# Routed attention and experts: the first pair loaded, turned and masked in halves, the key masks moved to ScalarE, and several experts' sums reordered

## The chip, the cores and the metric

The kernel runs on one core of a Trainium2 chip. The metric is the device time of one execution in microseconds, as the median of three runs. The engines are named as the profile names them: PE is TensorE (its weight loads are PEld), DVE is VectorE, ACT is ScalarE, POOL is GpSimd, and SP is SyncE, which here issues most of the DMAs.

## What is computed

Attention in which a query sees only the keys of its own cluster, followed by a layer of eight experts in which each token goes to one expert. The reference, cut to what matters:

```python
# q, k, v: (4, 8, 768, 64); centroids: (8, 16, 64)
q_n, k_n, c_n = (t / (np.linalg.norm(t, axis=-1, keepdims=True) + 1e-06) for t in (q, k, centroids))
q_assign = np.argmax(np.einsum('bhsd,hcd->bhsc', q_n, c_n), axis=-1)
k_assign = np.argmax(np.einsum('bhsd,hcd->bhsc', k_n, c_n), axis=-1)
mask = q_assign[:, :, :, None] == k_assign[:, :, None, :]
scores = np.where(mask, scale * np.matmul(q, k.transpose(0, 1, 3, 2)), -1000000000.0)
attn = softmax(scores)
x = np.matmul(attn, v)            # then (B,H,S,D) -> (3072 tokens, 512)
# experts: w_gate (512, 8), w1 (8, 512, 1024), w2 (8, 1024, 512)
expert_idx = np.argmax(x @ w_gate, axis=1)
y[token] = gate_w * (np.maximum(x[token] @ w1[e], 0.0) @ w2[e])   # e = expert_idx[token]
```

## The kernel before

The order of instructions on every engine is the order in which the program writes them (a manual schedule). Work that is to run beside other work is hung on hooks: `at_pair(n, u, f)` runs `f` after score step `u` of pair `n`, and in the experts `at(h1, i, f)` and `at(h2, i, f)` run `f` at hook `i` of layer 1 or layer 2 of stage `s`.

**Attention** goes over 16 pairs: a pair `n` is one batch and two heads, whose 2 x 64 dimensions fill the 128 partitions. For each pair:

- `load(n)` brings q and k. For pairs after the first it uses 128-byte pieces, in an order that lets DVE turn them in 32 x 32 blocks (`turn`, L277). Pair 0 is loaded by four DMAs on the SP and ACT queues (L183) in 256-byte pieces and is turned by 12 PE transposes into PSUM (L267), from where DVE and ACT copy it (`first_turn`, L282).
- `prepare(n, 1)` is `similar` (L312): the products of q and k with the normed centroids `cT`. `assign0`, `assign1` and `assign2` (L325 to L348) are seven DVE operations over 384 columns: turn, maximum, comparison, rank, maximum, comparison, turn. They end in `ohT`, the one-hot cluster of every query and key.
- `place` (L359, L361) spreads `ohT` into the masks: `mq` for queries by ACT copies, `mk` for keys by DVE, which multiplies by 2^60 and subtracts 2^60. Four instructions each, of 32 x 384.
- Twelve scores (`score`, L379, L392): for each half `h` of the queries and each block `j` of 128 keys, PE forms q times k in f32 (two passes, one of each head beside the other) and adds the bf16 product `mk` times `mq` to the same PSUM tile; ACT takes Exp of it. In pair 0 the first three raw products are issued before the first mask product. `add_up` (L398, DVE) sums the Exp tiles. There are three PSUM tiles for scores (`ps_s`) and two for everything else (`ps_m`).
- `attend` (L404): 24 products of the Exp tiles with v, then two ACT copies into `oT` (L411). `sum_up` (L427) for pair n runs at step 2 of pair n + 1, and so does `similar` for pair n + 2.

While a pair is computed, the next pair's `similar` is at step 2, `assign0` and `assign1` at 5, `assign2` at 7, `place` for keys at 8 and for queries at 11 (for pair 0's successor `similar` is at 4).

After the last pair of a batch the tokens are given to experts: `gate`, `gate_exp`, `choose`, `count` (L539 and L540: two f32 products with 128 x 128 constants of zeros and ones) and `number`, which scatters the tokens' rows by POOL (L554).

**Experts** run in ten stages (`s` from 0 to 9), each one expert's rows: layer 1 by Strassen-Winograd with 7 products for each of two halves (`layer1`, L916), layer 2 likewise for whole pairs of 128 rows (L1017), and directly for the rest (L1036). The sums that Strassen needs of weights (`w1_sums`, `w2_sums`) and of rows (`x_sums`, `h_sums`) are DVE operations of line L736; the additions that end a product are L874. For stage s + 1 and later ones: `places` reads the token list (`sf`) through SP, `indices` makes offsets of it on DVE, `gather` fetches rows by POOL (L685), `weigh` scales them on DVE (L702) and stores them, `take` reads them back, and `turn_rows` (L727) turns them. `ask` and `answer` check that all sums are in range.

## Time and profile before

| What | us |
|---|---|
| Median of three runs (lowest to highest) | 670.79 (670.62 to 671.94) |
| The profiled execution, its own time | 672.25 |
| Its span, first to last instruction | 670.7 |
| First PE instruction after the span's start | 5.24 |
| Attend of pair 0 begins | 27.32 |
| One ordinary pair, attend to attend | 19.74 |
| Last attend ends, experts begin | 336.5 |

The profile is of one execution, which took 1.5 us longer than the median. A group line names source line, engine and operation, what is written from what, how often, the busy time with the mean of one in ns, and the idle time of the engine just before it with what ended it. In a timeline the columns are start and length in us, engine, line and operation; brackets give the idle time ahead and its releaser. Ends of matmuls are modelled, so distances between starts are the better measure on PE.

### The profile page before, as it was taken

The numbers are of one execution on the slowest core, as the hardware profiler recorded it, in microseconds if no ns is written. First come the engines' busy times: TensorE is split into PE (matmuls) and PEld (weight loads), VectorE is DVE, ScalarE is ACT, GpSimd is POOL, SyncE is SP. The second block draws the span as 40 slices with busy tenths as digits, with TensorE's granted clock in tenths as the row PEclk, the third lists the DMA queues.
The fourth block names the chain that finished last, engine by engine and source line by source line (L and its number), as shares of the span: only waits on it lengthen the run. The fifth ranks groups of instructions, "written<-read, shape, count | busy, mean of one in ns | idle before, by whom it ended". The sixth has DMA issues, their size and how long they took to land.

```text
span 670.7 us, 11366 instructions
## 1 busy us (share of the span) xinstructions
PE 649.9 (97%) x4210; PEld 425.7 (63%) x4210; DVE 512.3 (76%) x901; ACT 300.0 (45%) x522; POOL 127.3 (19%) x156
## 2 busy tenths in 40 slices
PE   5999999999999999999999999999999999999995
PEld 2444444454444455444575879989798887969773
DVE  5889999999999999999886868878778366572300
ACT  3666556657556565556622333243332331423210
POOL 4100000012000300033104704225240422130010
PEclk9899999999999999999999989999999999999998
DMA  6843455433455443347475586685675844625010
GB/s 118 191 86 72 82 95 95 66 73 72 77 95 95 65 81 73 70 115 239 115 266 142 189 297 217 253 321 156 275 239 229 261 160 138 221 93 182 8 48 18
DMA packets 191806, 95.36 MB, mean 142 GB/s; under 512 B 155967, under 2 KB 173887, under 8 KB 190464
## 3 DMA queue, kind: packets, MB, share of 16 engines
q1 hardware_dynamic: 184560, 81.15, 44.0%
q0 software_dynamic: 4928, 12.97, 5.8%
q8 instruction: 35, 0.57, 0.4%
q10 hardware_dynamic: 2256, 0.44, 0.4%
q14 instruction: 27, 0.22, 0.1%
HBM read 74.10 MB, written 20.70 MB: 141 GB/s over the span
## 4 chain that ended last, share of the span: by engine, by line
PE 77%; issue 9%; DVE 7%; POOL 2%; DMA 2%; ACT 1%; POOLq 0%; SPq 0%; DVEq 0%; ACTq 0%
PE sps L379 20%; PE mps L404 15%; PE bank L916 9%; PE sbank L916 7%; PE bank L1017 7%; PE bank L1036 7%; PE sbank L1017 5%; PE mps L427 2%; PE mps L312 2%; DMA xg<-x_rows,gi 1%; PE bank L885 1%; DVE acc L398 1%; DVE v L736 1%; DVE xT L727 1%; POOL tokens_of L554 1%
## 5 line engine op out<-in xcount | busy, mean ns | idle before, releaser
L392 ACT ACTIVATE A<-sps 128x768 f32<-128x768 f32 x192 | 153.5, 811 | 44.9 <-PE sps L379 44.1
L379 PE MATMUL sps<-qT,kT 64*128 64x384 f32 x768 | 159.3, 494 | 0.6 <-ACT A L392 0.6
L398 DVE TENSOR_TENSOR acc<-acc,A 128x768 f32<-128x768 f32 x128 | 121.4, 948 | 10.1 <-ACT A L392 2.8
L404 PE MATMUL mps<-A,v_in 128*64 128x384 f32 x768 | 127.4, 488 | 0.0
L379 PEld LDWEIGHTS sps<-qT,kT 64*128 64x128 f32 x768 | 67.1, 188 | 55.0 <-issue 51.4
L404 PEld LDWEIGHTS mps<-A,v_in 128*64 128x64 f32 x768 | 53.8, 137 | 70.5 <-issue 61.7
L991 POOL DMA_INDIRECT out_dram<-z,si x30 | 47.6, 1587 | 198.4 <-DVE z L874 169.3
L554 POOL DMA_INDIRECT tokens_of<-tg,pos_i x24 | 26.7, 1111 | 281.9 <-DVE pos_i L552 148.2
L379 PE MATMUL sps<-mq,mk 64*128 64x384 bf16 x384 | 63.5, 325 | 2.6 <-DVE mk L361 2.6
L1036 PE MATMUL bank<-w,h 128*128 128x512 f32 (+2 forms) x224 | 64.4, 596 | 0.0
L685 POOL DMA_INDIRECT xg<-x_rows,gi x30 | 42.7, 1423 | 48.2 <-DVE si L676 18.1
L359 ACT COPY mq<-ohT 32x384 bf16<-32x384 bf16 x62 | 31.6, 510 | 42.7 <-DVE ohT L348 41.8
L916 PE MATMUL sbank<-xc,a 128*128 128x144 f32 (+4 forms) x288 | 48.0, 310 | 0.2
L916 PE MATMUL bank<-xT,w 128*128 128x144 f32 (+4 forms) x288 | 47.8, 309 | 0.0
L874 DVE TENSOR_TENSOR h<-sbank,p 128x288 f32<-128x288 f32 (+4 forms) x18 | 9.2, 512 | 48.3 <-PE sbank L916 48.3
L916 PEld LDWEIGHTS bank<-xT,w 128*128 128x128 f32 x288 | 43.8, 191 | 2.6 <-issue 2.2
L1036 PEld LDWEIGHTS bank<-w,h 128*128 128x128 f32 (+2 forms) x224 | 24.7, 152 | 32.5 <-issue 32.3
L916 PEld LDWEIGHTS sbank<-xc,a 128*128 128x128 f32 x288 | 43.3, 191 | 0.9 <-ACT sbank L940 0.6
L379 PEld LDWEIGHTS <-mk 64*128 64x128 bf16 x384 | 19.5, 95 | 28.0 <-DVE mk L361 3.4
L934 ACT ACTIVATE h<-h 128x288 f32<-128x288 f32 (+4 forms) x36 | 17.6, 488 | 42.7 <-DVE h L874 42.5
L702 DVE TENSOR_TENSOR xw<-xg,sf 128x256 f32<-128x256 f32 (+2 forms) x60 | 32.8, 606 | 1.8 <-DMA xg<-x_rows,gi 1.6
L398 DVE TENSOR_TENSOR acc<-A 128x768 f32<-128x768 f32 x32 | 30.2, 945 | 3.1 <-ACT A L392 2.9
(208 smaller groups left out, 890.7 us busy)
## 6 DMA issues: line engine op xcount, KB each, us to landing
w<-in_moe_w_dram SPq DMA_DIRECT2D x20, 2048.0 KB, 12.0
v_in<-in_v_dram SPq DMA_DIRECT2D x32, 192.0 KB, 2.8
x_rows<-x SPq DMA_DIRECT2D x64, 96.0 KB, 2.4
turn_rows<-xw SPq DMA_DIRECT2D x23, 256.0 KB, 2.0
q_in<-in_q_dram SPq DMA_DIRECT2D x60, 96.0 KB, 3.2
k_in<-in_k_dram SPq DMA_DIRECT2D x60, 96.0 KB, 3.2
xs<-turn_rows SPq DMA_DIRECT2D x16, 144.0 KB, 2.8
xs<-turn_rows SPq DMA_DIRECT2D x8, 208.0 KB, 4.2
```

Source lines behind the costliest of these rows:

```text
L359: (nc.gpsimd.tensor_copy if n == 0 and h else nc.scalar.copy)(dst, src)
L379: nc.tensor.matmul(SP[n, h, j][:, a, 0:HS], lhsT=kt[rows, j * P : (j + 1) * P], rhs=qt[rows, h * HS : (h + 1) * HS], start=first, stop=not ...
L392: nc.scalar.activation(A[n, h, j], ps[:, :, 0:HS], AF.Exp, scale=D**-0.5)
L398: nc.vector.tensor_tensor(ACC[n, h], first, A[n, h, j], op=ALU.add)
L404: nc.tensor.matmul(O[n, h][D * a : D * (a + 1), 0:HS], lhsT=VIN[n][:, a, j, :], rhs=A[n, h, j][:, a, :], start=(j == 0), stop=(j == NQ - 1),)
L554: ins = nc.gpsimd.indirect_dma_start(out=t_d[:, :], out_offset=bass.IndirectOffsetOnAxis(ap=pos_i[:, i : i + 1], axis=0), in_=tg[:, b, i, ...
L685: nc.gpsimd.indirect_dma_start(out=xg[0:m], out_offset=None, in_=x_d[0:rows_in, :], in_offset=bass.IndirectOffsetOnAxis(ap=g["gi"][0:m, j ...
L702: nc.vector.tensor_tensor(xw[0:m, :, :, d2 * a : d2 * (a + 1)], xg[0:m].rearrange("p (r a d b) -> p a r b d", r=HP, a=2, b=DB)[:, a], g["s ...
L916: nc.tensor.matmul(ps[:, f * T2 : (f + 1) * T2], lhsT=w[:, k, (2 * j + f) * P : (2 * j + f + 1) * P], rhs=x[:, k, :], start=first and f + ...
L991: ins = nc.gpsimd.indirect_dma_start(out=out[:, :], out_offset=bass.IndirectOffsetOnAxis(ap=GR[s]["si"][0:rows, j : j + 1], axis=0), in_=z ...
L1017: nc.tensor.matmul(ps[:, 0:H], lhsT=x[:, k, :], rhs=y[:, k, :], start=first and k == 0, stop=k == 3, skip_group_check=not first,)
L1036: nc.tensor.matmul(ps[i * m : (i + 1) * m, :], lhsT=h[:, f, j * P : j * P + m], rhs=w[:, f, :], start=(k == 0), stop=(k == FB // n - 1),)
```

## The change

Loading and turning pair 0: q and k come in four DMAs on SP's queue, the first half (of each partition's six rows) of q, of k, then the second halves, in pieces of 768 bytes. v of pair 0, the loads of pair 1 and the two small gate-weight loads follow on the same queue, ahead of the stores of `cT`, which used to be first. Six bf16 products of zeros are issued on PE before anything else. The halves are turned by products with the identity instead of transposes, copied by ACT alone, and clustered one after the other in chains over 192 columns. The masks of each half are placed by ACT, DVE and GpSimd together; GpSimd takes half of the key masks and most query masks. The three raw scores ahead are placed between the two halves.

All later pairs: the key masks are placed by ACT (Identity with a per-partition scale and bias) at step 11 instead of by DVE at step 8. Pair 1's preparation in pair 0 is moved to steps 6, 7, 8 and 11.

Counting: the constants and the operand are bf16 instead of f32.

Experts: the order of the `x_sums`, the hooks of some weight sums, of `places`, `ask` and `answer`.

The diff, cut to its core:

```diff
+        nc.gpsimd.tensor_copy(lt_b, lt_strict)
+        nc.gpsimd.memset(ones_b, 1.0)
...
-                if n == 0:
-                    t = d[n] = t.rearrange("p i d -> p (i d)").rearrange("p (j a d) -> p j a d", a=2, d=D)
-                    for a in range(2):
-                        (nc.sync, nc.scalar)[a].dma_start(out=t[:, :, a, :], in_=src[0, a].rearrange("(p j) d -> p j d", j=NQ))
-                    continue
...
+        def load_first():
+            for d, name in ((QIN, "q_in"), (KIN, "k_in")):
+                d[0] = ld.tile([P, NI, Q4], F32, name=name).rearrange("p i d -> p (i d)").rearrange("p (a j d) -> p a j d", a=2, d=D)
+            for h in range(2):
+                js = slice(NQ // 2 * h, NQ // 2 * (h + 1))
+                for d, src in ((QIN, q), (KIN, k)):
+                    nc.sync.dma_start(out=d[0][:, :, js, :], in_=src[0, 0:2].rearrange("a (p j) d -> p a j d", j=NQ)[:, :, js, :])
...
-        load(0)
+        load_first()
+        load_v(0)
+        load(1)
...
+        for t in (MQ[0], MK[0]):
+            nc.vector.memset(t, 0.0)
...
+        idle = ps_s.tile([P, 2, 512], F32, name="sps")
+        for _ in range(6):
+            nc.tensor.matmul(idle[:, 0, :], lhsT=MQ[0][:, 0:P], rhs=MQ[0][:, 0:512], start=True, stop=True)
...
-        warm = consts.tile([P, 1], F32)
-        nc.scalar.activation(warm, cnrm, AF.Exp, scale=0.0)
...
-            nc.scalar.dma_start(
+            nc.sync.dma_start(
...
-        nc.vector.tensor_tensor(cinv, cinv, cs2, op=ALU.mult)
-        nc.vector.tensor_tensor(cinv, cinv, cnrm, op=ALU.add)
+        nc.vector.tensor_scalar(cinv, cinv, scalar1=cs2[:, 0:1], scalar2=cnrm[:, 0:1], op0=ALU.mult, op1=ALU.add)
...
-        for d in (QIN, KIN):
-            ps = ps_s.tile([P, 2, 512], F32, name="sps")
-            t = d.pop(0)
-            for j in range(NQ):
-                c0 = P * (j % 3)
-                nc.tensor.transpose(ps[:, j // 3, c0 : c0 + P], t[:, j].rearrange("p a d -> p (a d)"), ident)
-            first.append(ps)
-            if d is QIN:
-                nc.tensor.transpose(cps[:, 0:P], cn.rearrange("p a d -> p (a d)"), ident)
...
-        first_turn(0)
-        cv = cps[:, 0:P].rearrange("p (h a c) -> p h a c", a=2, c=C)
-        for a in range(2):
-            nc.vector.tensor_copy(cT[D * a : D * (a + 1), :, a, :], cv[D * a : D * (a + 1), :, a, :])
...
-        load_v(0)
-        load(1)
-        first_turn(1)
...
+        def assign0(n, part=1):
+            sim = asg.tile([P, HI, 2 * C], F32, name="sim")[:, 0 : HI // part]
+            nc.vector.transpose(sim.rearrange("p i c -> p (i c)"), SIM.pop(n)[:, 0 : HS // part])
...
-            OH[n] = asg.tile([P, HS], BF16, name="ohT")
+            OH[n] = asg.tile([P, HS], BF16, name="ohT")[:, 0 : HS // part]
             nc.vector.transpose(OH[n], oh.rearrange("p i c -> p (i c)"))
...
                     if w == 0:
-                        (nc.gpsimd.tensor_copy if n == 0 and h else nc.scalar.copy)(dst, src)
+                        nc.scalar.copy(dst, src)
                     else:
-                        nc.vector.tensor_scalar(
-                            dst, src, scalar1=ksc2[Q4 * g : Q4 * (g + 1), a : a + 1],
-                            scalar2=kscn2[Q4 * g : Q4 * (g + 1), a : a + 1], op0=ALU.mult, op1=ALU.add,
-                        )
+                        big, less = (t[Q4 * g : Q4 * (g + 1), a : a + 1] for t in (ksc2, kscn2))
+                        nc.scalar.activation(dst, src, AF.Identity, bias=less, scale=big)
...
+        def start_first():
+            HQ = HS // 2
+            cps = ps_m.tile([P, 512], F32, name="mps")
+            ps = [ps_s.tile([P, 2, 512], F32, name="sps") for _ in range(2)]
+            src = [d.pop(0) for d in (QIN, KIN)]
+            dst = [qkt.tile([P, S], F32, name=name) for name in ("qT", "kT")]
+            QT[0], KT[0] = dst
+            def turned(w, h):
+                for j in range(NQ // 2):
+                    for a in range(2):
+                        nc.tensor.matmul(
+                            ps[w][D * a : D * (a + 1), h, P * j : P * (j + 1)], lhsT=src[w][:, a, NQ // 2 * h + j, :], rhs=ident,
+                            start=True, stop=True,
+                        )
+            def copied(w, h):
+                nc.scalar.copy(dst[w][:, HS * h : HS * (h + 1)], ps[w][:, h, 0:HS])
+            def similar_half(h):
+                sps = SIM[0] = ps_m.tile([P, 512], F32, name="mps")
+                for g in range(4):
+                    c0 = HS * h + HQ * (g % 2)
+                    nc.tensor.matmul(
+                        sps[Q4 * g : Q4 * (g + 1), 0:HQ], lhsT=cT[:, 0].rearrange("p a c -> p (a c)"),
+                        rhs=dst[g // 2][:, c0 : c0 + HQ], start=True, stop=True,
+                    )
+            def place_half(h, w):
+                for g in (2 * w, 2 * w + 1):
+                    for a in range(2):
+                        c0 = HS * h + HQ * (g % 2)
+                        to = (MQ, MK)[w][0][D * a : D * a + Q4, c0 : c0 + HQ]
+                        rows = slice(Q4 * g, Q4 * (g + 1))
+                        if w == 0:
+                            (nc.gpsimd.tensor_copy if h or g else nc.scalar.copy)(to, OH[0][rows])
+                        else:
+                            (nc.gpsimd if g % 2 else nc.vector).tensor_scalar(
+                                to, OH[0][rows], scalar1=ksc2[rows, a : a + 1], scalar2=kscn2[rows, a : a + 1],
+                                op0=ALU.mult, op1=ALU.add,
+                            )
+            def clusters(h):
+                assign0(0, 2)
+                assign1(0, 2)
+                assign2(0, 2)
+                for w in (h, 1 - h):
+                    place_half(h, w)
+            turned(0, 0)
+            copied(0, 0)
+            turned(1, 0)
+            copied(1, 0)
+            warm = consts.tile([P, 1], F32)
+            nc.scalar.activation(warm, cnrm, AF.Exp, scale=0.0)
+            nc.tensor.transpose(cps[:, 0:P], cn.rearrange("p a d -> p (a d)"), ident)
+            cv = cps[:, 0:P].rearrange("p (h a c) -> p h a c", a=2, c=C)
+            for a in range(2):
+                nc.vector.tensor_copy(cT[D * a : D * (a + 1), :, a, :], cv[D * a : D * (a + 1), :, a, :])
+            turned(0, 1)
+            copied(0, 1)
+            similar_half(0)
+            turned(1, 1)
+            copied(1, 1)
+            clusters(0)
+            score_half(0, 0, 0, True)
+            similar_half(1)
+            for j in (1, 2):
+                score_half(0, 0, j, True)
+            clusters(1)
+            OH.pop(0)
+            for a in range(2):
+                nc.sync.dma_start(
+                    out=cn_d.rearrange("(h a) d c -> a d h c", a=2)[a], in_=cT[D * a : D * (a + 1), :, a, :]
+                )
...
-            ahead = range(3) if n + h + j == 0 else (j,) if n + h or j > 2 else ()
-            for i in ahead:
-                score_half(n, h, i, True)
+            if n + h or j > 2:
+                score_half(n, h, j, True)
...
-            last = LAST[b] = rt.tile([P, E], F32, name="last")
+            last = LAST[b] = rt.tile([P, E], BF16, name="last")
...
-            nc.tensor.matmul(cps[:, 0:E], lhsT=lt_strict, rhs=last, start=True, stop=True)
-            nc.tensor.matmul(cps[:, E : 2 * E], lhsT=ones_sq, rhs=last, start=True, stop=True)
+            nc.tensor.matmul(cps[:, 0:E], lhsT=lt_b, rhs=last, start=True, stop=True)
+            nc.tensor.matmul(cps[:, E : 2 * E], lhsT=ones_b, rhs=last, start=True, stop=True)
...
+            strassen(V, X[2], b22, b12, ALU.subtract)
             strassen(V, X[0], b12, b11, ALU.subtract)
             strassen(V, X[1], b22, X[0], ALU.subtract)
-            strassen(V, X[2], b22, b12, ALU.subtract)
             strassen(V, X[3], b21, X[1], ALU.subtract)
...
-            for u, step in ((2 if n else 4, 1), (5, 2), (7, 3), (8, 4), (11, 5)):
+            for u, step in ((2 if n else 6, 1), (5 if n else 7, 2), (7 if n else 8, 3), (11, 4), (11, 5)):
...
-        for step in range(1, 6):
-            prepare(0, step)
+        start_first()
...
+                at(h2, 5, places, 3)
...
             if s == 3:
-                at(h1, 5, ask)
-                at(h1, 9, answer)
+                at(h1, 12, ask)
+                at(h2, 4, answer)
...
-                if 2 < s + 2 <= last:
-                    places(s + 2)
...
+                if 0 < s <= last - 3:
+                    at(h2, 1, places, s + 3)
...
                 if s == 0:
-                    when = ((h2, 1), (h2, 2), (h2, 4), (h2, 5), (h2, 7), (h2, 7))
+                    when = ((h2, 1), (h2, 2), (h2, 5), (h2, 6), (h2, 7), (h2, 7))
                 elif s == 1:
-                    when = ((h1, 9), (h1, 10), (h2, 2), (h2, 3), (h2, 6), (h2, 6))
+                    when = ((h1, 9), (h1, 12), (h2, 2), (h2, 3), (h2, 6), (h2, 6))
...
-                at(h1, 6, w2_sums, s, (3,), nc.vector)
+                at(h1, 5 if s == 1 else 6, w2_sums, s, (3,), nc.vector)
```

## The prediction

> **What bounds the kernel.** I read the busy shares first, then who PE waited for, then the chain in order of time, then timelines of the places that the chain and the waits name. The page says PE is the engine to follow:
> ```profile
> PE 649.9 (97%) x4210; PEld 425.7 (63%) x4210; DVE 512.3 (76%) x901; ACT 300.0 (45%) x522; POOL 127.3 (19%) x156
> ```
> The waits of PE alone (engine, what it would write, whom it waited for, sum, times, longest):
> ```profile
> PE sps L267 <- POOL first_cb L301: 5.2, 1, 5.2
> PE sbank L916 <- DVE h L874: 3.4, 3, 2.4
> PE sps L379 <- DVE mk L361: 2.6, 2, 2.4
> ```
> So three places matter: the start, the first masks, and layer 1 of the experts. (The 5.2 us ended with the landing of q, issued on ACT's queue at 1.24 with 3.9 us to landing; POOL had been ready before.) The chain in order of time (start, length, what) shows the steady state:
> ```profile
> 8.45 2.19 PE mps L312 x8
> ...
> 27.32 7.89 PE mps L404 x48
> ...
> 47.06 7.89 PE mps L404 x48
> ...
> 66.80 7.89 PE mps L404 x48
> ...
> 137.65 1.18 PE mps L312 x8
> ```
> From one pair's attend (L404) to the next is 19.74 us, and PE has no wait in it: an ordinary pair can't get shorter by serving PE better. But pair 0's attend begins only at 27.32. The cluster products (L312) cost 2.19 us there against 1.18 later. The timeline of the first masks:
> ```profile
> 10.67 0.58 DVE L325 STREAM_TRANSPOSE sim<-mps 128x384 f32<-128x384 f32 x1 [1.62 <-PE mps L312]
> ...
> 14.12 0.58 DVE L348 STREAM_TRANSPOSE ohT<-oh 128x384 bf16<-128x384 bf16 x1
> 14.73 1.04 ACT L359 COPY mq<-ohT 32x384 bf16<-32x384 bf16 x2 [5.76 <-DVE ohT L348]
> ```
> Seven DVE operations in a row take 10.67 to 14.70; PE idles from 13.0 to 15.42. By stretch (span; then busy of PE, PEld, DVE, ACT, POOL; granted clock, DMA), the clock then falls:
> ```profile
> 11.20:18.00 6.80, 3.63 (x24) 1.50 (x22) 6.12 (x12) 2.67 (x5) 2.93 (x11) 1.00 0.92 169
> 18.00:21.50 3.50, 3.50 (x20) 1.03 (x16) 2.84 (x4) 2.08 (x3) 2.21 (x29) 0.51 1.00 342
> ```
>
> [...](1) [...]0.51 for 3.4 us after the idle stretch, and 2.19 against 1.18 us above. (2) [...]q's 192 KB in 256-B pieces land 3.9 us after issue, v's 192 KB in 1,536-B pieces 2.8. (3) [...]L359 with 384 elements measures 510[...]. (4) [...]Copies and Exps alternate here with only two table loads in the trace, both before 5.4.
>
> **A. The start.** Removed: 256-B first loads, 12 transposes, one cluster chain over 384 columns. Added: 6 zero products, 24 transposing products (two passes each), two chains over 192 columns.
> - Zeros: DVE's memset of mq (0.38) moves to the front, done near 1.15[...].
> - Loads: SP issues four at 0.8, 1.5, 2.15, 2.8 (0.65 apart, as L183 now), landing 2.8 later by v's row: 3.6, 4.3, 4.95, 5.6, against 5.1 (q) and 6.8 (k). v of pair 0, pair 1 and wgt queue behind them; ACT loses three q, k and wgt issues, so Sqrt runs near 3.2 instead of 3.89. wgt now lands after pair 1's loads, and is not needed before 31.
> - One half of q or k is 6 products, two side by side: [...]q half 3.8-5.1, k half to 5.75, ACT copies (0.48) to 5.7 and 6.4, cT (two DVE copies) to 6.55, cluster products of half one to 7.05. The Exp table load (1.28) now sits behind k's first copy on ACT: the copies of half two end at 8.4 and 8.9, and nobody needs them before DVE is through with chain one. The fused cinv step (0.2) is ahead of none of this.
> - Chain on DVE at half width: transposes 0.38 (slt's row with 192 columns), the other five some 0.25-0.36 by halving what is above a fixed 0.15-0.2: 2.65. ohT one at 9.8 instead of 14.70.
> - Masks one: ACT 2 x 0.35, DVE 2 x 0.3, GpSimd 4 serial. Its 32x384 copy is 0.49; the two-pointer form is not in the trace: 0.3 to 0.7, I take 0.4, so to 11.4. Chain two starts on DVE at 10.4, ends at 13.0; DVE's masks to 13.7, GpSimd's k to 13.9, its four q by 15.3, needed only from score 6.
> - PE: three raw scores ahead fit in 7.7-10.6; masks 0-2 follow from 10.6; score 3 waits for DVE's mask until 13.7. From there 8 scores x 0.81 (Exp's pace) + similar(1) 0.64 + 0.4: attend at **21.3** instead of 27.32, 6.0 us.
> - Taken back: PE is 60% idle from 10.6 to 13.7, so the clock may fall again: 3.4 us at half, 1.7 lost, even chance: 0.8. DVE, now late with 2 turns, 10 adds and pair 1's chain, gives ohT(1) at 26.8; with the new placing (C) its mask waits 0.5. **A = -4.7**, from -6.5 to -1.5.
>
> **B. bf16 counts, and DVE 1.5 us lighter per pair.** GpSimd's two new constants (a copy and a memset, 0.3) lie in routing_constants, long before the first count. In pairs 6, 10, 13 the period is 20.8 to 21.4. Timeline: L539/L540 from 138.76 to 139.30, 0.54; in bf16 one pass and short loads, about 0.22: 4 x 0.32 = 1.3. There k's cluster products also start 0.5 after q's, as kT came late from DVE (137.94); without four L361 (4 x 0.38) ahead it comes in time: 3 x 0.5. **B = -2.8** (-3.3 to -1.2).
>
> **C. k's masks from DVE to ACT (15 pairs).** The transition, pair 5 to 6:
> ```profile
> 128.87 0.58 DVE L348 STREAM_TRANSPOSE ohT<-oh 128x384 bf16<-128x384 bf16 x1
> ...
> 134.59 0.33 PE L379 MATMUL sps<-mq,mk 64*128 64x384 bf16 x2
> ```
> From ohT to the first mask product there are 5.1 us (4.6 to 5.7 over the pairs; 2.5 for pair 14). ACT would need 4 x 0.70 ([...]between 0.51 and 0.81, Exp's row) + 2 x 0.52 = 3.85 before that mask can go, 4.9 for all. Behind them queue both oT copies (0.96), a gate Exp, and the next pair's first Exp, at 5.85 after ohT, up to 1.25 after the first mask; PE asks for that buffer 3.7 after it. ACT's load grows from 12.6 to 15.4 of 19.7. So nothing in ordinary pairs (0.3 allowed); cover gone, each 0.1 costs 1.5 over the kernel. Pair 14: 1.3 late, against 0.9 that sum_up waited there for acc at 298.5 and no longer has to, and 0.4 of late kT. **C = +0.3** (-0.8 to +3).
>
> **D. Experts.** The biggest wait, stage 1 of layer 1:
> ```profile
> 382.52 1.21 DVE L736 TENSOR_TENSOR v<-w,v 128x1024 f32<-128x1024 f32 x1
> 383.65 1.22 DVE L736 TENSOR_TENSOR a<-w 128x1024 f32<-128x1024 f32 x1
> 384.97 1.23 DVE L736 TENSOR_TENSOR a<-w,a 128x1024 f32<-128x1024 f32 x1
> 386.11 0.45 DVE L874 TENSOR_TENSOR h<-sbank,p 128x288 f32<-128x288 f32 x1
> ...
> 386.62 2.27 PE L916 MATMUL sbank<-xT,a 128*128 128x144 f32 x8 [2.42 <-DVE h L874]
> ```
> v(3) goes ahead of xw (which waits for its gather anyway), a(1) goes behind h: h at 383.8, the wait is gone (-2.3). x_sums earlier by a 1.2 us w1 sum, and X[2] first: 0.4 at 372.2. ask/answer away from stage 3's layer 1: their 1 us of DVE leaves ahead of L874, 0.55 at 442.1. places one stage earlier: sf, waited for at 493.7 by DVE, 0.26 at 497.8. SP passes the same DMAs, ahead of take and second_weights instead of between; both have slack. Waits of 0.2 to 0.4 at 483.9, 555.8, 597.1 stay (xT ahead of z). Sum -3.5; I take **-3.3** (-4.2 to 0), as a(1) could now be late for the next sums.
>
> **Sum.** -4.7 - 2.8 + 0.3 - 3.3 = -10.5. The profiled execution took 672.25 (span 670.7), 1.5 above the median of 670.79; so 661.8 by its own time, **660.3** as a median.
>
> **Rivals.**
> 1. Clock: zeros don't raise it in time, or it falls again. For: 18.0-21.5. Against: five continuous us before. A = -2.3: 662.7. Chance 0.2.
> 2. Experts' waits move on (h_sums or xT late instead). For: DVE's sum there is unchanged. D = -0.8: 662.8. Chance 0.14.
> 3. The change doesn't split the start: half one waits for the whole (dependencies, or k's late landing). Two chains then follow each other, 5.3 against 4.0: A = 0: 665. Chance 0.07.
> 4. Slower: ACT becomes the bound at each pair's end. If Identity displaced Exp's set, every pair would get two loads. At the 1.28 of the trace, the mask path is 5.1 and Exp late by 0.3 a pair: still 665. [...]It decides from a mask path of 5.9 (10.5/15 = 0.7 beyond the mean slack of 5.2). Against it: point (4). Chance 0.06.
>
> **Numbers.** The forecast has 0.53 (656.5 to 663). Under 0.2% (1.34 us) nothing could be told from no change. Range 656.5 to 666.5 takes in rivals 1 to 3. Faster 0.91 (the first four cases), same 0.03 (the upper end of rival 3), slower 0.06 (rival 4).
>
> **What would show it.** First attend at 21-23; ohT one near 10; L312-like products in one step in pairs 6, 10; PE's wait for h near 0.5 instead of 3.4; two table loads; the ordinary pair still 19.7. It is wrong if ordinary pairs exceed 20, or the first attend is after 25.

## The result, and the profile after

The changed kernel takes **659.65 us** (median of six runs, 658.82 to 660.05), the kernel before 671.16 in the same session (six runs, 670.62 to 672.79): a ratio of 0.9823, 95% interval 0.9811 to 0.9836, or 11.5 us less. 660.3 had been forecast. The sum came out; two of its four terms did not, and the runs below show that their errors cancelled.

The profiled execution after took 659.27 us (span 657.5), against 672.25 (span 670.7). The page after, busy time of each engine and the clock row:

```profile
PE 644.2 (98%) x4252; PEld 423.3 (64%) x4252; DVE 490.0 (75%) x845; ACT 338.8 (52%) x584; POOL 130.8 (20%) x166
...
PEclk9999999999999999999999999999999999999999
```

DVE lost 22 us and ACT gained 39 (the key masks). The clock row of the page before was:

```profile
PEclk9899999999999999999999989999999999999998
```

Three of its slices showed an 8: the second, the twenty-fourth (386 to 402 us) and the last, behind PE's last work; now none does. PE's waits after (same columns as before):

```profile
PE sps L226 <- DVE mq L219: 1.4, 1, 1.4
PE sps L433 <- ACT mq L337: 1.3, 2, 1.1
PE sbank L1069 <- DVE z L926: 1.2, 4, 0.4
PE sbank L968 <- DVE h L926: 1.0, 3, 0.7
PE sps L433 <- DVE mk L383: 1.0, 1, 1.0
```

5.2 us ahead of the first product became 1.4, the 2.4 for the first masks became 1.0, and of the waits for `h` (L916 before, L968 now; 3.4 in all) 1.0 is left, the longest 0.7 instead of 2.4; new is 1.1 us for ACT's query masks (pair 14). The chain in order of time:

```profile
1.39 2.74 PE sps L226 x6
4.13 2.67 PE sps L356 x24
...
19.75 4.24 PE sps L433 x30
23.99 7.89 PE mps L457 x48
43.73 7.89 PE mps L457 x48
```

The first attend (L404 before, L457 now) is at 23.99 instead of 27.32, not at 21.3; an ordinary pair is still 19.74. Between the same points of the two first profiles PE's work moved up like this (before minus after, by the first product of each):

| Point | before | after | gained so far |
|---|---|---|---|
| attend of pair 0 | 27.25 | 23.92 | 3.3 |
| attend of pair 15 | 328.59 | 321.58 | 7.0 |
| layer 1 of stage 1 | 370.83 | 362.98 | 7.9 |
| layer 1 of stage 2 | 403.81 | 392.12 | 11.7 |
| layer 1 of stage 4 | 457.35 | 444.81 | 12.5 |
| PE's last end | 663.93 | 651.15 | 12.8 |

The periods of the pairs that carry a count went from 20.81, 20.82 and 21.42 to 19.88 each, pair 14's from 21.73 to 21.53.

Where the start lost 2.7 us on the forecast, the timeline after shows:

```profile
4.06 1.55 PE L356 MATMUL sps<-ident,q_in 128*64 128x128 f32 x12
5.39 1.40 PE L356 MATMUL sps<-ident,k_in 128*64 128x128 f32 x12
...
8.39 0.38 DVE L302 STREAM_TRANSPOSE sim<-mps 128x192 f32<-128x192 f32 x1 [0.82 <-PE mps L368]
...
10.73 0.38 DVE L327 STREAM_TRANSPOSE ohT<-oh 128x192 bf16<-128x192 bf16 x1
...
11.22 0.82 DVE L383 TENSOR_SCALAR mk<-ohT,ksc,kscn 32x192 bf16<-32x192 bf16 x2
12.07 0.38 DVE L302 STREAM_TRANSPOSE sim<-mps 128x192 f32<-128x192 f32 x1
12.07 1.10 POOL L383 TENSOR_SCALAR mk<-ohT,ksc,kscn 32x192 bf16<-32x192 bf16 x2
...
14.59 0.38 DVE L327 STREAM_TRANSPOSE ohT<-oh 128x192 bf16<-128x192 bf16 x1
...
15.38 0.70 PE L433 MATMUL sps<-mq,mk 64*128 64x384 bf16 x2 [1.01 <-DVE mk L383]
```

The halves do work apart, and a chain takes 2.72 (8.39 to 11.11; 2.65 forecast). But both first halves were turned cold, 1.55 and 1.40 us, so chain one began at 8.39 instead of 7.1; a mask takes 0.41 on DVE instead of 0.3 (0.55 on GpSimd instead of 0.4), so chain two, behind DVE's two masks, began at 12.07 and not at 10.4. From the first mask product of score 3 to the attend it is 8.5 us (15.38 to 23.92), where the forecast had 7.6.

The cold halves are in part the luck of this one execution. The trace's own record of the clock begins at the moment when the products become fast: here at 6.57, between a half of 1.40 us (at 5.39) and one of 0.88 (at 6.98), and in the eight other profiles of kernels with the zero products at 4.29 to 6.10 (mean of the nine 5.4). In those eight chain one begins at 7.51 to 8.16.

### The profile page after: what moved, and what is told of

It is laid out like the page before. It is cut to its first block, busy times and chain, and to the rows that moved or that the text cites. A ratio compares the mean times of both kernels' runs of the same rounds, so it can differ in the third digit from the quotient of the medians.

```text
span 657.5 us, 11491 instructions
## 1 busy us (share of the span) xinstructions
PE 644.2 (98%) x4252; PEld 423.3 (64%) x4252; DVE 490.0 (75%) x845; ACT 338.8 (52%) x584; POOL 130.8 (20%) x166
## 4 chain that ended last, share of the span: by engine, by line
PE 80%; issue 10%; DVE 5%; POOL 2%; ACT 1%; DMA 1%; POOLq 0%; DVEq 0%; ACTq 0%
PE sps L433 20%; PE mps L457 16%; PE bank L968 10%; PE sbank L968 8%; PE bank L1069 7%; PE bank L1088 7%; PE sbank L1069 6%; PE mps L480 2%; PE mps L291 1%; PE bank L937 1%; DMA xg<-x_rows,gi 1%; DVE xT L780 1%; POOL tokens_of L607 1%; DVE acc L451 1%; DVE a L789 1%
## 5 line engine op out<-in xcount | busy, mean ns | idle before, releaser
L457 PE MATMUL mps<-A,v_in 128*64 128x384 f32 x768 | 127.4, 488 | 0.0
L457 PEld LDWEIGHTS mps<-A,v_in 128*64 128x64 f32 x768 | 53.7, 137 | 70.6 <-issue 62.9
L433 PE MATMUL sps<-mq,mk 64*128 64x384 bf16 x384 | 64.9, 323 | 3.1 <-ACT mq L337 1.3
L340 ACT ACTIVATE mk<-ohT,kscn,ksc 32x384 bf16<-32x384 bf16 x60 | 42.0, 700 | 40.5 <-DVE ohT L327 39.7
L968 PE MATMUL bank<-xT,w 128*128 128x144 f32 (+4 forms) x288 | 47.7, 309 | 0.0
L738 POOL DMA_INDIRECT xg<-x_rows,gi x30 | 38.4, 1280 | 47.0 <-DVE si L729 16.4
L968 PE MATMUL sbank<-xc,a 128*128 128x144 f32 (+4 forms) x288 | 47.7, 309 | 0.0
L968 PEld LDWEIGHTS bank<-xT,w 128*128 128x128 f32 x288 | 43.8, 190 | 2.6 <-issue 2.2
L968 PEld LDWEIGHTS sbank<-xc,a 128*128 128x128 f32 x288 | 43.4, 190 | 0.0
```

What stands on the lines that cost most here:

```text
L340: nc.scalar.activation(dst, src, AF.Identity, bias=less, scale=big)
L433: nc.tensor.matmul(SP[n, h, j][:, a, 0:HS], lhsT=kt[rows, j * P : (j + 1) * P], rhs=qt[rows, h * HS : (h + 1) * HS], start=first, stop=not ...
L457: nc.tensor.matmul(O[n, h][D * a : D * (a + 1), 0:HS], lhsT=VIN[n][:, a, j, :], rhs=A[n, h, j][:, a, :], start=(j == 0), stop=(j == NQ - 1),)
L738: nc.gpsimd.indirect_dma_start(out=xg[0:m], out_offset=None, in_=x_d[0:rows_in, :], in_offset=bass.IndirectOffsetOnAxis(ap=g["gi"][0:m, j ...
L968: nc.tensor.matmul(ps[:, f * T2 : (f + 1) * T2], lhsT=w[:, k, (2 * j + f) * P : (2 * j + f + 1) * P], rhs=x[:, k, :], start=first and f + ...
```

## The experiments

Each median is of five or six runs (fourteen for e6). The last three columns are of one profiled execution each: first product of the first attend, of the last pair's attend, and PE's last end.

| Kernel | us, median (range) | ratio to before (95%) | first attend | last attend | PE end |
|---|---|---|---|---|---|
| e0_after_again | 660.69 (658.60 to 662.84) | 0.9837 (0.9812 to 0.9862) | 24.07 | 321.73 | 652.84 |
| e10_after_third | 660.51 (658.90 to 662.31) | 0.9846 (0.9826 to 0.9865) | 23.39 | 321.04 | 650.52 |
| e1_no_zeros | 661.09 (658.86 to 661.37) | 0.9835 (0.9810 to 0.9859) | 24.08 | 321.74 | 652.86 |
| e2_old_start | 660.21 (658.93 to 660.88) | 0.9822 (0.9797 to 0.9848) | 27.25 | 324.52 | 652.80 |
| e11_old_start_again | 659.99 (658.73 to 660.57) | 0.9831 (0.9813 to 0.9849) | 26.54 | 323.87 | 650.61 |
| e3_keys_dve | 663.24 (662.68 to 666.22) | 0.9881 (0.9855 to 0.9907) | 23.64 | 324.68 | 654.77 |
| e4_f32_counts | 661.21 (660.05 to 662.12) | 0.9842 (0.9815 to 0.9869) | 23.69 | 322.56 | 653.12 |
| e5_old_experts | 666.82 (664.88 to 667.55) | 0.9922 (0.9899 to 0.9945) | 24.41 | 322.05 | 659.36 |
| e6_fill_wait (on before) | 671.14 (670.20 to 673.39) | 0.9999 (0.9987 to 1.0011) | 27.46 | 329.62 | 665.16 |
| e9_both | 657.52 (657.44 to 659.07) | 0.9803 (0.9780 to 0.9825) | 22.23 | 319.27 | 649.27 |
| e12_stage1_only | 660.84 (659.97 to 662.62) | 0.9847 (0.9826 to 0.9868) | 23.45 | 321.11 | 652.59 |
| e13_masks_dve | 662.02 (659.74 to 662.56) | 0.9856 (0.9834 to 0.9877) | 24.75 | 322.08 | 653.01 |

e1 to e4 ran on one chip, e0, e5, e6 and e9 on a second, e10 to e13 on a third; differences are taken within a group where the changed kernel ran in it. It did not run beside e1 to e4: there the times can only be set beside those of other chips, and the stages of the profiles say more. Before had 671.84, 671.49 and 671.49 on the three.

### The start: e2_old_start, e11_old_start_again, e1_no_zeros, e13_masks_dve

**e2_old_start and e11_old_start_again** are one kernel, run twice: the start of the kernel before (loads, their order and queues, transposes, one chain, no zeros, pair 1's old steps), all else as changed. Cut to two places, and written as a step from the changed kernel:

```diff
-        load_first()
+        load(0)              # 256-B pieces, SP and ACT queues
...
-        start_first()
+        for step in range(1, 6):
+            prepare(0, step)
```

> The changed kernel with the start of the kernel before (256-B loads, 12 transposes, one chain over 384 columns, no zeros); counts, keys' masks on ACT from pair 1 and experts as changed. Theory: all that the new start gives is what the first attend shows, 27.25 against 23.92: time +3.3 us against the changed kernel. The prediction's size: +4.7. Rival: pair 1's clusters come late after the split start and give part back, so that the old start costs less than 3.3, say +2.

> The old start with everything else as changed, beside the changed kernel on one chip (its first run stood within 1 us of it, though its attention ended 2.8 us later). Theory A: what the new start gives is lost in the experts' part, where rows and weights land at their own pace and PE's waits grow by what it comes sooner: time within 1 us of the changed kernel, and its stretch from the last pair's attend to PE's end is 2 to 3 us shorter than the changed kernel's. Theory B: the stretches differ by chance from run to run (landings 1.1 us earlier or later), and over several runs the start's gain stands: time +2 to +3.3 us.

The changed kernel beside it was e10_after_third (and e0_after_again in another group):

> The changed kernel itself once more, as the measure for the three beside it. Expected 659.5 to 661, first attend 23.9 to 24.1.

> The changed kernel itself, as the measure for the three beside it on this chip. Expected within 1 us of 659.65. If the experts' part is one where waits on landing weights come and go from run to run, its profile shows the wait in layer 1 of stage 3 near 429 (0.4 to 1.0 us in the four kernels tried so far, none in the first profile of the changed kernel).

e10 missed its range: its first attend is at 23.39, because its clock came up at 5.46 and not at 6.57. From the start of chain one to the first attend it is 15.5 us in all six profiles of this start in which the clock then held (the first, e1, e3, e4, e10, e12). The wait of stage 3 that e0 looks for was there (0.79 us at 429.10).

Theory A of e11 holds. The old start attends 3.15 us later than e10, and its time is 659.99 against 660.51; from the last pair's attend to PE's end it is 2.7 us shorter: **what the start gains over the old one is not there at the end.** Over both pairs of profiles (e10 and e11 ran on one chip, and both profiled runs are the fastest of their five; e0 and e2 ran on two chips):

| Changed kernel ahead of the old start by, us | e10 against e11 | e0 against e2 |
|---|---|---|
| attend of pair 0 | 3.15 | 3.18 |
| attend of pair 15 | 2.83 | 2.79 |
| layer 2 of stage 0 | 1.22 | 1.43 |
| layer 2 of stage 1 | 1.23 | 0.41 |
| layer 2 of stage 3 | 0.44 | 0.31 |
| PE's end | 0.09 | -0.04 |

The largest single loss, 1.4 to 1.6 us, is in stage 0. There DVE waits for the turned rows, whose write to memory (L761) and read back (L771) SP issues during the last pair. The timeline of e10_after_third:

```profile
310.98 2.45 SPq L761 DMA_DIRECT2D turn_rows<-xw  x3
317.35 1.83 SPq L771 DMA_DIRECT2D xs<-turn_rows  x4
321.85 1.38 DVE L780 STREAM_TRANSPOSE xT<-xs 128x1152 f32<-128x1152 f32 x1 [2.46 <-DMA xs<-turn_rows]
```

and of e11_old_start_again (the same three lines, numbered by its own source):

```profile
313.81 2.43 SPq L717 DMA_DIRECT2D turn_rows<-xw  x3
318.93 1.82 SPq L727 DMA_DIRECT2D xs<-turn_rows  x4
323.40 1.38 DVE L736 STREAM_TRANSPOSE xT<-xs 128x1152 f32<-128x1152 f32 x1 [1.16 <-DMA xs<-turn_rows]
```

From write to read back it is 6.37 us in one and 5.12 in the other, and DVE has its sums and `h` later by that. The packet records tell the two apart: in the changed kernel one 16-KB packet of the instruction queue (0.88 us long) falls just ahead of the write's end. The write's last two packets of 2 KB follow as it ends, one behind the other, and the last ends 0.43 us after it (in the first profile the packet lies from 315.83 to 316.71, and the two last ones, of 0.23 us each where the others take 0.08, end at 316.92 and 317.13). That holds for all eight profiles in which such a packet falls there (the changed kernel three times, e4, e5, e9, e12, e13: read back 6.2 to 6.5 after the write's issue in each); in the six others it falls earlier (e3), as the write ends (e1) or not near it (before, e2, e6, e11), and the read back comes at 5.0 to 5.3. It is a match in the records of fourteen profiles: no run moved the packet on purpose, and how one packet could hold up the whole write was not shown.

The next loss is in a load of weights that lands no sooner. In stage 2 DVE has a lead of 1.23 us in e10 over e11 up to a weight sum. There e10 waits for the load and e11 does not, and the lead is 0.07 (first line e10, second e11):

```profile
410.27 1.23 DVE L789 TENSOR_TENSOR v<-w 128x1024 f32<-128x1024 f32 x1 [1.21 <-DMA w<-in_moe_w_dram]
410.34 1.22 DVE L745 TENSOR_TENSOR v<-w 128x1024 f32<-128x1024 f32 x1
```

PE's lead then falls in stage 3, from 1.22 to 0.44. e1, set beside e0 across two chips, shows the same with more at stake: its rows were read back after 5.24 us, and it entered layer 2 of stage 2 1.7 us ahead of e0. DVE then waited for the weights, PE waited 1.30 us for its `z`, and at layer 1 of stage 3 the lead is 0.1:

```profile
412.50 1.22 DVE L786 TENSOR_TENSOR v<-w 128x1024 f32<-128x1024 f32 x1 [3.12 <-DMA w<-in_moe_w_dram]
```

So the loss does not hang on the packet alone. The rest of it (pair 14's 0.3, 1.0 in stage 1 of e0, and 0.35 where PE waits for `z` of a DVE that has no pause) has no single cause that was isolated.

**e1_no_zeros:** the six zero products left out.

```diff
-        idle = ps_s.tile([P, 2, 512], F32, name="sps")
-        for _ in range(6):
-            nc.tensor.matmul(idle[:, 0, :], lhsT=MQ[0][:, 0:P], rhs=MQ[0][:, 0:512], start=True, stop=True)
```

> The changed kernel without its six zero products; nothing else differs. Theory: PE gets its full clock some 5.3 us after its first product, whatever that product is (5.24 to about 10.6 in the kernel before, 1.39 to about 6.8 in the changed one). Without the zeros the first product is at about 4.1, so all four halves of q and k and both sets of cluster products run cold: similar half one ends near 9.2 instead of 8.3, ohT one near 12.0 instead of 11.1, first attend near 24.8 instead of 23.9, time +0.8 us. Rival: the zeros do nothing (the clock rises when the transposing products have run for a while anyway, and DVE is what the start waits for): first attend within 0.2 of 23.9, time within 0.3 us.

Beside the first profile of the changed kernel the rival looks right: chain one begins at 8.62 instead of 8.39, 0.2 us later, and the first attend is at 24.08. But that profile had the latest clock of nine. In e1 the record of the clock begins at 7.51, against a mean of 5.4 with the zeros, and chain one begins 0.7 later than the mean of 7.9 with them. With one profile of e1, in which the clock came up 3.7 us after the first product, against 2.9 to 5.2 with the zeros and 2.9 to 6.0 in the kernels with the old start, what the zeros are worth stays open. The theory's fixed lead of 5.3 us did fall. That the zeros can raise the clock is shown by e0: there it came up at 4.29, when PE had run only them (1.39 to 4.06) and a first 0.2 us of turning, and the first half of q took 0.97 us instead of 1.55:

```profile
4.06 0.97 PE L356 MATMUL sps<-ident,q_in 128*64 128x128 f32 x12
```

**e13_masks_dve:** all of the first pair's key masks on DVE.

```diff
-                            (nc.gpsimd if g % 2 else nc.vector).tensor_scalar(
+                            nc.vector.tensor_scalar(
```

> The changed kernel with all eight key masks of the first pair on DVE, none on GpSimd. Theory: chain two starts two masks of 0.41 later, so score 3 waits 0.8 longer for its first mask, less 0.15 since DVE's compare no longer runs beside a GpSimd op (0.51 instead of 0.36): first attend 24.5 to 24.8 (+0.6 to +0.8). Rival: GpSimd's masks of 0.55 are what the scores wait for, then first attend is at 23.9 or sooner.

First attend at 24.75, 1.36 later than e10, time 662.02 against 660.51. From the end of ohT one to score 3's first mask 4.95 us pass instead of 4.27, the expected 0.7. The other half of the loss was not expected. By stretch (columns as in the prediction's stretches), e13_masks_dve:

```profile
13.00:15.00 2.00, 0.42 (x4) 0.00 (x0) 1.73 (x6) 0.88 (x2) 0.21 (x1) 1.00 0.42 81
15.00:17.00 2.00, 1.76 (x6) 1.01 (x8) 1.87 (x5) 0.81 (x1) 1.74 (x7) 0.53 0.09 9
17.00:18.00 1.00, 1.00 (x6) 0.79 (x4) 1.00 (x2) 0.25 (x1) 0.93 (x6) 0.50 0.06 22
```

PE's idle time is one piece of 1.82 us here, and the clock falls for 3.4 us behind it. In the changed kernel the slow GpSimd masks (0.55 us each) spread PE's products and the wait is 1.0. Even so the clock of the same kernel fell in e0_after_again and not in e10_after_third, with equal waits:

```profile
13.00:15.00 2.00, 1.00 (x7) 0.24 (x4) 1.73 (x6) 1.24 (x2) 0.71 (x2) 0.88 0.53 122
15.00:17.00 2.00, 2.00 (x9) 1.46 (x10) 2.00 (x3) 0.81 (x2) 1.80 (x5) 0.50 0.12 13
```

That is e0; e10, same stretches:

```profile
13.00:15.00 2.00, 1.00 (x8) 0.32 (x4) 1.73 (x6) 1.51 (x2) 0.47 (x1) 1.00 0.66 147
15.00:17.00 2.00, 1.97 (x16) 1.37 (x17) 1.97 (x4) 1.43 (x2) 1.70 (x6) 1.00 0.15 17
```

From chain one to the first attend it is 16.56 us in e0 and 16.75 in e5, the other profile with a fall, against 15.5: a fall at this place costs 1.0 to 1.2 us.

### Masks and counts: e3_keys_dve, e4_f32_counts

```diff
-                        nc.scalar.activation(dst, src, AF.Identity, bias=less, scale=big)
+                        nc.vector.tensor_scalar(dst, src, scalar1=..., scalar2=..., op0=ALU.mult, op1=ALU.add)
...
-            ... (7 if n else 8, 3), (11, 4), (11, 5)):
+            ... (7 if n else 8, 3), (8 if n else 11, 4), (11, 5)):
```

> The changed kernel with the keys' masks of pairs 1 to 15 on DVE again, at the place in the order where the kernel before had them. Theory: DVE's 1.5 us a pair come back, kT is late again in pairs 6, 10 and 13: their periods are 20.3 to 20.4 instead of 19.88 (+1.5 together); in pair 14 the 1.1 us wait for ACT's queries goes and 0.7 us for acc returns; time +1.0 to +1.8. Rival: kT is in time for another reason (the earlier end of the start, the steps' new places), then the three periods stay at 19.9 and the time is 0.3 to 0.5 lower than the changed kernel's.

From first to last attend it took 301.04 us instead of 297.66: +3.4, twice what was expected, at 663.24. The three periods with a count are 20.43, 20.42 and 21.02, and the pairs behind them are late too (20.18, 20.08, 19.97). Pair 14 has 21.66.

```diff
-            last = LAST[b] = rt.tile([P, E], BF16, name="last")
+            last = LAST[b] = rt.tile([P, E], F32, name="last")
...   (and the products' constants lt_strict and ones_sq)
```

> The changed kernel with the counts' products in f32 again. Theory: each count takes 0.4 us more on PE (0.54 instead of the 0.14 by which pairs 6, 10 and 13 exceed 19.74): four counts, +1.6; periods 20.3 in those pairs. The prediction's size: 0.32 each, +1.3. Rival: the excess of 1.07 in the kernel before was nearly all late kT, and a count's own products lie beside others: +0.3 in all, periods 19.95.

As the theory had it: the three periods are 20.28 instead of 19.88, 0.40 each. First to last attend is 1.2 longer, the time 661.21. The time alone does not part it from the changed kernel's. e3 and e4 together give 4.6, more than the 3.7 between before and after. In the three periods with a count the two add up to what before and after differ by (0.55 and 0.40 against 0.93 in the first); what is over lies in the pairs behind, 1.0 late in e3, 0.5 in e6 (whose attention is that of the kernel before) and only 0.06 in the first profile of the kernel before. So that part comes and goes, and e3's 3.4 may count up to 0.9 too much.

### The experts: e5_old_experts, e12_stage1_only, e6_fill_wait

**e5_old_experts** undoes every edit of that part (x_sums, `when`, `places`, `ask` and `answer`, `w2_sums` 3).

```diff
-                    when = ((h1, 9), (h1, 12), (h2, 2), (h2, 3), (h2, 6), (h2, 6))
+                    when = ((h1, 9), (h1, 10), (h2, 2), (h2, 3), (h2, 6), (h2, 6))
...
-                at(h1, 5 if s == 1 else 6, w2_sums, s, (3,), nc.vector)
+                at(h1, 6, w2_sums, s, (3,), nc.vector)
...   (and the other edits of the change's last hunks)
```

> The changed kernel with everything in the experts' part in the old order (x_sums, when, places, ask and answer, w2_sums 3). Theory: the 2.4-us wait of PE for h in stage 1 is back, and it costs more than itself, since the granted clock falls to a half behind it for 3.5 us, as it did in the kernel before (386.6 to 390): 2.4 + 1.6, with 0.5 to 1 for the waits of stage 3: time +4 to +5 against the changed kernel. The prediction's size: +3.3, the waits alone. Rival: landings of weights bound these stages, so that most of what one wait gives another takes: +2 or less.

+6.1 us against e0 (666.82 and 660.69): more than the theory, nearly twice the prediction. The profiled run is the slowest of its six. PE's waits and the stretch behind the longest of them:

```profile
PE sbank L968 <- DVE h L926: 4.5, 4, 2.6
...
PE bank L968 <- DVE xc L789: 1.3, 1, 1.3
```

```profile
380.00:381.00 1.00, 0.53 (x2) 0.53 (x3) 0.41 (x2) 0.55 (x2) 0.00 (x0) 0.77 0.27 66
381.00:383.00 2.00, 2.00 (x10) 1.91 (x9) 0.46 (x1) 0.85 (x3) 0.00 (x0) 0.50 0.73 213
383.00:384.00 1.00, 1.00 (x4) 0.82 (x3) 0.79 (x2) 0.18 (x1) 0.00 (x0) 0.53 0.96 180
```

The wait of 2.57 is followed by 3.4 us at half clock, in which PE was busy throughout: by the granted 0.50, half of that, 1.7, is lost (an estimate; e6 below measures 1.7 at such a place). By stage, from layer 1 to the next layer 1, e5 is longer than e0 by 4.5 in stage 1, 0.6 in stage 2, 1.0 in stage 3, and by nothing from there on.

**e12_stage1_only** undoes only the two lines shown above.

> The changed kernel with two places of the experts' order undone, both of stage 1: the w1 sum a(1) of the next stage ahead of h again, and this stage's w2 sum v(3) later. Theory: of the 6 us that the whole old order cost, the 2.4-us wait and the 3.5 us at half clock behind it are here: +3.5 to +4.5. Rival: the wait comes back without the clock's fall, or later waits shrink by as much: +2.5 or less. Second rival: the other edits carry most of the 6 (x_sums' order and places): +1 or less.

Its wait is 1.08 us, not 2.6, and the clock doesn't fall. Stage 1 is 2.1 longer than in e10 (0.7 and 1.3 longer than in e0 and the first profile), but the time is only 0.3 above (660.84 and 660.51); e10's profiled run was its fastest. The theory fell. The size is the second rival's, and the wait came back without the clock's fall, as the first has it: the 2.6-us wait needs other edits of that part too. How the 6.1 us divide among them stays open.

**e6_fill_wait** is the kernel before with PE kept busy in its 2.4-us wait.

```diff
+                if s == 1 and j == 1:
+                    idle = bank()
+                    for _ in range(10):
+                        nc.tensor.matmul(idle, lhsT=ones_sq.bitcast(BF16)[:, 0:P],
+                            rhs=first_cb[:, None, :].to_broadcast([P, 512 // C, C]), start=True, stop=True)
                 product(c, A[3], b22)
```

> The kernel before, unchanged but for ten bf16 products of ones (512 columns, 2.2 us) on PE in the 2.4-us wait of stage 1, into a bank that nobody reads. Theory: the wait for h ends at the same moment, but PE was busy through it, so the granted clock stays at 1.00 where it had been 0.50 to 0.84 from 386 to 390: products of that stage in 1.14 instead of 2.27 us, time -1.6 us against the kernel before. Rival: the clock falls for another reason (power, the DMA load), or what follows waits for DVE's sums anyway: -0.3 or less; or the products hold up h and the time rises.

The stretches of before, with the clock at 0.50:

```profile
387.00:388.00 1.00, 1.00 (x6) 1.00 (x6) 0.46 (x1) 0.48 (x3) 0.00 (x0) 0.50 0.91 255
388.00:389.00 1.00, 1.00 (x5) 1.00 (x5) 0.00 (x0) 0.38 (x2) 0.00 (x0) 0.50 0.70 194
```

and of e6:

```profile
387.00:388.00 1.00, 0.63 (x4) 0.42 (x4) 0.53 (x2) 0.44 (x2) 0.00 (x0) 1.00 0.59 160
388.00:389.00 1.00, 1.00 (x9) 0.97 (x8) 0.46 (x1) 0.47 (x3) 0.00 (x0) 1.00 0.84 243
389.00:390.00 1.00, 1.00 (x7) 0.87 (x6) 0.41 (x1) 0.56 (x2) 0.00 (x0) 1.00 0.89 201
```

`h` comes at the same moment of the stage, the clock stays up, and stage 1 takes 31.25 us instead of 32.98. So the clock's fall costs 1.7 us at that place, and its cause is PE's idleness and not the load elsewhere. The time is nevertheless unchanged. In stage 2 a wait appears that before didn't have:

```profile
416.55 1.16 PE L916 MATMUL sbank<-xT,a 128*128 128x128 f32 x8 [1.67 <-DVE h L874]
```

DVE's three weight sums (1.2 us each) stand ahead of that `h`. They begin at 412.49, where before had 411.26, since DVE pauses twice ahead of them: 1.05 us for a small load, and 1.33 us for which the trace shows no reason. PE reached the stage 0.7 sooner than before (its start had been 1.0 later), DVE did not: the second half of the expectation's rival. The profiled run took 673.21, 2 us over the median of its fourteen, so it shows where the gain can go, not that it went there in each.

### A version faster than both: e9_both

```diff
+                            if h == 0 and g % 2 == 0:
+                                nc.scalar.activation(to, OH[0][rows], AF.Identity, bias=kscn2[rows, a : a + 1], scale=ksc2[rows, a : a + 1])
+                                continue
...
+            elif n == NPAIR - 2:
+                if step == 4:
+                    for w, h in ((1, 0), (0, 0), (1, 1)):
+                        place(n, w, (h,))
...
+        at_pair(NPAIR - 2, 3, place, NPAIR - 2, 0, (1,))
```

> The changed kernel with two more edits: of the first pair's first half, DVE's two key masks go to ACT, so that chain two starts on DVE at 11.2 instead of 12.07; and in pair 14 ACT places first the half of the keys and of the queries that the first mask product reads, and the queries' other half only at score 3. Theory: both waits are of placing, the rest has room: first attend 23.0 to 23.3 instead of 23.92, pair 14's period 20.3 to 20.5 instead of 21.53; time -1.5 to -2.0 us. Rival: the experts' part takes part of it back (their weights land no sooner): attention ends 1.9 earlier, time -1.0 or less. Second rival: ACT is then late with the first three Exps, first attend not before 23.8.

657.52 against e0's 660.69: 3.2 less, more than expected; the two ratios' intervals just overlap, and beside the three ratios of the changed kernel (0.9823 to 0.9846) e9's 0.9803 is 1.3 to 2.9 us less. First attend 22.23, sooner than expected; pair 14's period 20.91, which missed 20.3 to 20.5. PE's waits for masks:

```profile
PE sps L436 <- ACT mk L384: 0.8, 2, 0.6
PE sps L436 <- ACT A L448: 0.7, 2, 0.4
```

The 1.0-us wait for DVE's mask is gone and the clock stays up, which e0's did not. Here the lead lasts: e9 reaches the last attend 2.5 us ahead of e0 and 1.8 ahead of e10, and PE's end 3.6 and 1.25 ahead. So not every gain ahead of the experts is lost in them; which part of one is kept, no run settles.

## Why the prediction was right, and where its steps were wrong

**A, the start (-4.7): the mechanism came, the size did not, and the gain did not last.** 3.3 us at the first attend, where the forecast's own timeline had 6.0, or 5.2 with its 0.8 for the clock. When the clock comes up in the new start and what a half costs until then were the author's estimates, not read from the trace of before: the forecast's timeline had both first halves turned by 5.75, the first profile at 6.79. Its clock came up at 6.57, against a mean of 5.4 over nine: there it had bad luck. "0.4" for a GpSimd mask was 0.55, 0.3 on DVE 0.41, and DVE's two put chain two a further 0.3 behind; the stretch from score 3 to the attend was put 0.9 too short. "Even chance" of the clock's falling was high: two of the eight profiles with the new masks (e0 and e5), at 1.0 to 1.2 us and not 1.7. Pair 1's mask did not wait (0.5 allowed). The step that failed outright is a silent one: that a microsecond gained ahead of the first attend is still there at the end. e2 and e11 put A at about nothing, and the traces show rows and weights that land no sooner.

**B and C, counts and key masks (-2.8 and +0.3): right, a little small.** 3.7 us between first and last attend. A count saves 0.40, not 0.32. DVE's lighter load was priced by kT alone (1.5), where e3 shows 3.4: 2.2 in the three periods, 1.0 in the pairs behind them, where it comes and goes. The mask on ACT takes 700 ns, as forecast:

```profile
L340 ACT ACTIVATE mk<-ohT,kscn,ksc 32x384 bf16<-32x384 bf16 x60 | 42.0, 700 | 40.5 <-DVE ohT L327 39.7
```

Ordinary pairs bore it. Pair 14's mask came 1.1 late (1.3 forecast), and the waits it replaces made the pair 0.2 shorter.

**D, the experts (-3.3): too small by nearly half.** 6.1 by e5, 4.9 to 5.8 by the first profiles (from layer 1 of stage 1, or from the last attend). The wait of 2.4 was counted at 2.3. What stood behind it was not: 3.4 us at half clock, which the page before showed as the second 8 in its clock row, 1.7 by e6. The prediction read the clock of the start and not of this stage. No wait of PE for a(1) appeared in the profile after.

**Rivals.** The first (the clock) happened in some executions. The second (waits that move on) was put at the wrong step: it is A's gain that went into later waits. The third ended near the truth for A, but not by its mechanism: the halves are split. The fourth did not come: two table loads, periods of 19.74. Of its sizes only the 665, from the 1.28 us of a table load, had the trace behind it; that the kernel could become slower was the author's estimate.

So the total was right by luck, through errors of opposite sign: A gave some 4.7 us less than forecast, B to D some 4 more (3.7 and 6.1 instead of 2.5 and 3.3). Those come to 9.8 of the 11.5 us; parts undone one at a time need not add up, and the rest is not assigned.

## What to carry to other kernels

A gain at the start is worth what is left of it at the last instruction: look for the later places where another engine or a transfer keeps its own pace (here the rows' way through memory and a load of weights), and do not count it whole beyond the next of them. e9, whose lead lasted, shows that it need not be lost either. Price a wait of PE with the clock behind it (here 1.7 us more behind one of 2.4), and read the clock row of the page before adding up waits. Where the order of work on one queue decides, ask first which half of an operand the next instruction reads (e9).

## What the runs showed of the hardware

- The granted clock fell to 0.50 for 3.41 us (6.83 in e6's start) behind PE waits of 2.3 to 2.7 us in every profile that had one at masks or at `h` and no products in it (before twice, e2, e11, e6's start, e5's stage 1), behind 1.8 in e13, and behind 1.0 in two of eight profiles of one pattern. In before, e0 and e5 the falls lie on steps of 3.413 us. Counted from the moment at which the trace's record of the clock begins, the falls of before at 18.04 and 386.68 (record from 11.22) begin after 2.00 and 110.01 such steps and last one each, and that of e0 at 14.52 (record from 4.29) begins after 3.00; the two of e5, at 15.30 and 380.54, are 107.0 steps apart. Of such steps at full clock, over the fourteen profiles, those that PE's products filled to 0.21 to 0.49 (busy time, with modelled ends) all brought a fall, none above 0.62 did, and between the two some did (0.53 to 0.62) and some did not (0.51 to 0.62): in before the step from 11.22 was filled to 0.54 and brought none, the next one, to 0.54 as well, did, and so did the one from 383.2, filled to 0.29. So a wait of 1.0 us cost a fall in e0 and an equal one none in e10.
- At the very start the stretch view gives a clock of 1.00 while products take 1.55 us that later take 0.88: the record begins only when the clock comes up (6.57 in after), so the cold start doesn't show in that column. It came up 2.9 to 6.0 us after the first product.
- A 16-KB packet of the instruction queue, one every 11 to 31 us through most of the kernel, takes 0.88 to 1.7 us, and in all eight profiles where one fell just ahead of the end of a 0.6-MB write, that write ended 0.43 us after it (after: 316.71 and 317.13).
- DVE's comparison of 192 columns took 0.51 us beside a GpSimd mask (after, at 12.87; e10) and 0.36 without one (e13, at 12.78).
